# Other opening and drain of attention, gates in every second couple, and where the 64-bit conversions stand: a change to a fused attention and two-stage feed-forward kernel

## The chip, the cores and the metric

The kernel runs on one core of one Trainium2 chip. A core has a matrix engine (TensorE, PE in the profile, its weight loads apart as PEld), a vector engine (VectorE, DVE), a scalar engine (ScalarE, ACT), GpSimd (POOL) and a queue that mostly issues transfers (SyncE, SP). Each works through its own instructions in order and waits for the others through semaphores. SBUF is the working memory, PSUM takes TensorE's results. The metric is the device time of one execution, in microseconds (us).

## What is computed

Inputs are q, k, v (4 batches, 8 heads, 576 positions, head size 64), the weights of a mixture of 8 experts, and w_in and w_out, which arrive as 64-bit floating point numbers.

```python
scores = where((rel >= 0) & (rel < 128), scale * q @ k.T - slope[h] * abs(rel), -1e9)
attn   = exp(scores - max) / (sum + 1e-9);   x = attn @ v            # (2304, 512)
P      = exp(x @ w_gate - max);  8 times: P /= P.sum(1); P /= P.sum(0); P *= 2304 / 8
x      = sum over e of P[:, e] * (relu(x @ w1[e]) @ w2[e])           # 512 -> 1024 -> 512
h      = x @ w_in;   out = (h * cos(h)) @ w_out                      # 512 -> 2048 -> 512
```

## The kernel before

The program is one function, whose instructions are issued in an order written out by hand. Three stages follow each other.

**Attention** works on 16 pairs of heads. A pair has five groups of 128 queries (the last of 64), so there are 80 groups, and two groups that follow each other form a couple: 40 couples. In turn i of the loop (line 793) PE gets the scores of couple i (`emit_qk`, L537 and L535), then the products of couple i-4 (`emit_AV`, L639), transposes of q and k of the next pair (`emit_T`, L494) and the transposes of the probabilities of couple i-3 (`emit_PT`, L601 and L603). DVE takes the row maxima (`emit_max`, L547), ACT the exponentials (`emit_exp`, L562) and the copies of the transposed probabilities (L614), POOL normalizes (`emit_norm`, L586), and `emit_x` copies the finished x of a pair out of PSUM (L655 on DVE for odd pairs, L657 on ACT for even ones). PSUM has two score banks (`ps_s`), three banks for transposes (`ps_t`), one for gates and for the first halves of q and k (`ps_g`), and a double bank `xbank` for the products, whose second part the second halves of q and k use too. Couples 1 and 3 put half of their scores into `xbank`. Everything follows in program order on each engine; a buffer or a bank that is taken again makes the writer wait for its last reader.

Beside this, `side` spreads other work over the groups: `load_f64` and `convert_f64` (L260 to L279, five operations on DVE and one on ACT) turn a 128x512 piece of the 64-bit weights into fp32, one step a group; `prep_s`, `prep_a`, `prep_b` and `prep_sb` split expert weights into a high and a low part; `stages` and `combos` prepare the operands of the first expert block. `gates` puts the products x @ w_gate of 384 tokens (`gate_block`, L371) and, a turn later, their transposition by a matmul and the copy into `logits` (`gate_block2`, L380 and L381) into the loop. `load_heads` issues the loads of q, k and v on SP's queue.

**Three expert blocks** of 768 tokens follow, with 32 units each (8 experts times 4 slices). The products are a seven-product scheme: a unit computes its seven in the order 5, 1, 4, 2, 3, 6, 7 (`product`, L966); in the first block, the products with w2 of the unit before stand ahead of 7 (`batch`, L1194 to L1196, into the banks gT0 to gT2, evacuated by DVE). After each product and each tile, `slot` takes one step of every list of waiting work: `sbq` (here `prep_sb`, with POOL sums L181, an ACT copy L184, a DVE split L186), `bg` (late gates, then the normalization of P, `sinkhorn`, L389 to L423) and others. The first block starts with the late gates and `sinkhorn`, whose small matmuls (L393, L399, L417) stand among PE's products. **Three blocks of the last layer** end the program.

The conversions that attention doesn't take stand in `bg` of the second and third expert block.

## Time and profile before

| | us |
|---|---|
| median of 3 runs (lowest, highest) | 1987.18 (1985.54, 1992.14) |
| the profiled execution | 1983.78 |
| its span, first to last instruction | 1982.0 |

| engine | busy us | share of the span |
|---|---|---|
| PE | 1958.4 | 99% |
| PEld | 1823.2 | 92% |
| DVE | 1559.7 | 79% |
| ACT | 862.2 | 44% |
| POOL | 967.0 | 49% |

The profile is one execution. A row of the timeline gives the start, the duration, engine, line, operation, what is written and read by the program's names, and in brackets how long the engine was idle ahead of it and what released it. A matmul's end is modelled, so a busy PE isn't PE at its peak. A wait for several things is put down to the one that came last. Attention runs from 6.0 to 156.1 us.

### The profile page before, as it was taken

The numbers are of one execution on the slowest core, as the hardware profiler recorded it, in microseconds if no ns is written. First come the engines' busy times: TensorE is split into PE (matmuls) and PEld (weight loads), VectorE is DVE, ScalarE is ACT, GpSimd is POOL, SyncE is SP. The second block draws the span as 40 slices with busy tenths as digits, with TensorE's granted clock in tenths as the row PEclk, the third lists the DMA queues.
The fourth block names the chain that finished last, engine by engine and source line by source line (L and its number), as shares of the span: only waits on it lengthen the run. The fifth ranks groups of instructions, "written<-read, shape, count | busy, mean of one in ns | idle before, by whom it ended". The sixth has DMA issues, their size and how long they took to land.

```text
span 1982.0 us, 31160 instructions
## 1 busy us (share of the span) xinstructions
PE 1958.4 (99%) x10977; PEld 1823.2 (92%) x10977; DVE 1559.7 (79%) x2669; ACT 862.2 (44%) x1617; POOL 967.0 (49%) x939
## 2 busy tenths in 40 slices
PE   8999999999999999999999999999999999999999
PEld 6667899999999999999999999999999999998898
DVE  7885877777777788988988877888877776757766
ACT  6885444444444433333333433333233354554543
POOL 5673566666667545454536622545454523333221
PEclk9999999999999999999999999999999999999999
DMA  7854788888888999999999888999898765565552
GB/s 195 220 141 159 263 311 292 309 303 313 310 289 310 319 340 316 343 338 317 340 327 328 274 281 284 330 341 335 324 308 296 242 222 196 197 218 176 207 192 96
DMA packets 293755, 540.05 MB, mean 272 GB/s; under 512 B 80256, under 2 KB 141792, under 8 KB 286432
## 3 DMA queue, kind: packets, MB, share of 16 engines
q1 hardware_dynamic: 292240, 537.74, 78.6%
q8 instruction: 87, 1.43, 0.3%
q14 instruction: 68, 0.56, 0.1%
q10 hardware_dynamic: 1360, 0.33, 0.1%
HBM read 384.32 MB, written 153.67 MB: 271 GB/s over the span
## 4 chain that ended last, share of the span: by engine, by line
PE 88%; DVE 2%; DMA 1%; issue 0%; SPq 0%; POOL 0%; ACT 0%; ACTq 0%; DVEq 0%; POOLq 0%
PE gT L1105 23%; PE y_moe L966 19%; PE z_moe L966 10%; PE gT L1195 7%; PE gT L1196 7%; PE gT L1194 7%; PE y_ffn L966 5%; PE x_moe L966 5%; PE z_ffn L966 2%; PE x_ffn L966 1%; DMA wbX<-wdp 1%; SPq L96 0%; DVE waX L145 0%; DVE acc_ffn L1175 0%; DVE ta L939 0%
## 5 line engine op out<-in xcount | busy, mean ns | idle before, releaser
L1105 PE MATMUL gT<-hX,wbX 128*128 128x384 f32 x2688 | 538.3, 334 | 0.9 <-DMA wbX<-wdp 0.5
L1105 PEld LDWEIGHTS gT<-hX,wbX 128*128 128x128 f32 x2688 | 471.7, 188 | 3.5 <-DMA wbX<-wdp 1.5
L966 PE MATMUL y_moe<-xtT_moe,waX 128*128 128x384 f32 x1728 | 347.1, 335 | 0.6 <-ACT s_moe L995 0.6
L966 PEld LDWEIGHTS y_moe<-xtT_moe,waX 128*128 128x128 f32 x1728 | 304.3, 188 | 3.7 <-ACT s_moe L995 0.9
L1117 DVE TENSOR_TENSOR acc_moe<-gT,acc_moe 128x384 f32<-128x384 f32 x432 | 237.7, 550 | 77.7 <-PE gT L1105 76.0
L1196 PE MATMUL gT<-wbX,hX 128*128 128x512 f32 x660 | 258.0, 391 | 0.0
L1195 PE MATMUL gT<-wbX,hX 128*128 128x512 f32 x660 | 257.8, 391 | 0.0
L1194 PE MATMUL gT<-wbX,hX 128*128 128x512 f32 x660 | 257.7, 390 | 0.0
L995 ACT ACTIVATE s_moe<-y_moe 128x384 f32<-128x384 f32 x192 | 93.3, 486 | 345.6 <-PE y_moe L966 345.5
L1139 POOL TENSOR_TENSOR hodd<-hodd 128x384 f32<-128x384 f32 x128 | 155.4, 1233 | 139.4 <-DVE hX L1125 70.4
L1139 POOL TENSOR_TENSOR cX<-cX 128x384 f32<-128x384 f32 x128 | 146.6, 1165 | 153.6 <-DVE hX L1125 93.8
L955 POOL TENSOR_TENSOR hX<-cX,hX 128x768 fp32r<-128x768 f32 x44 | 83.5, 1914 | 249.3 <-ACT hX L952 208.6
L132 POOL TENSOR_TENSOR s<-ra 128x256 f32<-128x256 f32 x80 | 62.4, 780 | 251.3 <-DVE waX L145 178.9
L1185 DVE SCALAR_TENSOR_TENSOR acc_moe<-gT,prob,acc_moe 128x512 f32<-128x512 f32 x174 | 129.6, 747 | 37.6 <-PE gT L1196 35.8
L1196 PEld LDWEIGHTS gT<-wbX,hX 128*128 128x128 f32 x660 | 123.8, 188 | 26.0
L1194 PEld LDWEIGHTS gT<-wbX,hX 128*128 128x128 f32 x660 | 123.9, 188 | 25.4 <-DVE acc_ffn L1175 0.6
L1195 PEld LDWEIGHTS gT<-wbX,hX 128*128 128x128 f32 x660 | 123.9, 188 | 24.5
L911 ACT ACTIVATE hX<-cX 128x768 fp32r<-128x768 f32 x64 | 44.0, 687 | 218.7 <-DVE cX L998 218.7
L1125 DVE TENSOR_TENSOR hX<-cX,hX 128x768 fp32r<-128x768 f32 x112 | 132.4, 1182 | 1.1 <-ACT hX L1129 1.1
L1125 DVE TENSOR_TENSOR hX<-hodd,hX 128x768 fp32r<-128x768 f32 x112 | 127.5, 1138 | 0.9 <-ACT hX L1129 0.9
L966 PE MATMUL z_moe<-xtT_moe,waX 128*128 128x384 f32 x576 | 116.4, 335 | 0.4 <-DVE waX L145 0.2
L966 PE MATMUL z_moe<-xtB_moe,waX 128*128 128x384 f32 x576 | 115.9, 335 | 0.0
(210 smaller groups left out, 3771.9 us busy)
## 6 DMA issues: line engine op xcount, KB each, us to landing
waX<-wd SPq DMA_DIRECT2D x264, 512.0 KB, 5.5
wbX<-wdp SPq DMA_DIRECT2D x224, 512.0 KB, 6.5
wd<-waX SPq DMA_DIRECT2D x32, 1792.0 KB, 6.8
wdp<-sb SPq DMA_DIRECT2D x32, 1024.0 KB, 5.8
wdp<-wbX SPq DMA_DIRECT2D x96, 256.0 KB, 4.4
wbX<-wd SPq DMA_DIRECT2D x24, 1024.0 KB, 4.8
waX<-wd SPq DMA_DIRECT2D x88, 256.0 KB, 5.2
ra<-in_moe_w_dram SPq DMA_DIRECT2D x64, 256.0 KB, 7.4
```

What stands on the lines that cost most here:

```text
L132: nc.gpsimd.tensor_tensor(out=s4[:, o], in0=x, in1=y, op=op)
L955: eng.tensor_tensor(out=h[:, 1], in0=c, in1=h[:, 0].bitcast(F32), op=ALU.subtract)
L966: nc.tensor.matmul(ps[:, :HB], wa[:, WI[m], wl, kc, :], x[:, xl, kc, :], start=start and kc == 0 and n_ == 0, stop=stop and kc == 1 and n_ ...
L995: nc.scalar.activation(out=t["s", i], in_=ps[:, :HB], func=AF.Copy)
L1105: nc.tensor.matmul(ps[:, :HB], w[:, u, wl, d * P:(d + 1) * P], x[:, xl, u, :], start=m in (1, 5, 2) and n_ == 0, stop=m in (4, 3, 2) and n ...
L1117: nc.vector.tensor_tensor(out=a, in0=ps[:, :HB], in1=a, op=ALU.add)
L1125: nc.vector.tensor_tensor(out=x[:, 1], in0=H[:, q], in1=x[:, 0].bitcast(F32), op=ALU.subtract)
L1139: nc.gpsimd.tensor_tensor(out=H[:, t[0], c], in0=H[:, t[1], c], in1=H[:, t[2], c], op=ALU.subtract)
L1185: nc.vector.scalar_tensor_tensor(out=a, in0=ps, scalar=pe, in1=a, op0=ALU.mult, op1=ALU.add)
L1194: nc.tensor.matmul(ps, hf[f][:, 0, ts], wb[:, f, 0, :], start=f == 0, stop=False)
L1195: nc.tensor.matmul(ps, hf[f][:, 0, ts], wb[:, f, 1, :], start=False, stop=False)
L1196: nc.tensor.matmul(ps, hf[f][:, 1, ts], wb[:, f, 0, :], start=False, stop=f == 1)
```

## The change

- **Opening.** Couple 1's scores take two banks of `ps_t`, couple 3's the ordinary score banks; neither uses `xbank`. In turn 0 the loads of q and k of pair 2 are issued, and the v loads of pairs 0 and 1 move behind them; afterwards q and k are loaded for pair + 3 instead of pair + 2. In turn 3 `emit_PT` stands right behind the gates, ahead of `emit_AV` and the transposes of q and k.
- **Drain.** In turns 41 to 43 `emit_PT` stands ahead of `emit_AV` too. In the last four groups the second head and the last, short group are normalized by DVE. The copies behind the transposes of groups 77 and 79 go to DVE. The last pair's x is copied half by ACT, half by DVE.
- **Gates.** A turn does either `gate_block2` or the next `gate_block`, not both.
- **Conversions.** None in attention (four before). Six stand in units 4 to 23 of the first expert block, one step behind each of the products 5, 1 and 7. 26 instead of 28 are left for the next two blocks.
- **`prep_sb(0)`** moves from the last turns of attention to the head of `sbq` in the first expert block.

```diff
@@ -522,10 +522,8 @@
         def emit_qk(n, pi, u):
             a = n % 2
             if n // 2 not in sbank:
-                if n // 2 in (1, 3):
-                    sbank[n // 2] = [xbank[:, :512], ps_t.tile([P, 512], F32, tag="t", name=f"s{n}_1")]
-                else:
-                    sbank[n // 2] = [ps_s.tile([P, 512], F32, tag="s", name=f"s{n}_{j}") for j in range(2)]
+                pool, tag = (ps_t, "t") if n // 2 == 1 else (ps_s, "s")
+                sbank[n // 2] = [pool.tile([P, 512], F32, tag=tag, name=f"s{n}_{j}") for j in range(2)]
             grp[n] = sbank[n // 2] if a == 0 else sbank.pop(n // 2)
             c0, c1 = span(u)
             k0 = (u - 1) * P + c0
@@ -583,7 +581,8 @@
                 c0, c1 = span(u)
                 for j in parts(u):
                     pt = grp[n][j]
-                    nc.gpsimd.tensor_scalar(
+                    eng = nc.vector if n >= NGR - 4 and (j or u == NG - 1) else nc.gpsimd
+                    eng.tensor_scalar(
                         out=pt[:, c0:c1], in0=pt[:, c0:c1], scalar1=rr[:, i:i + 1],
                         scalar2=1.0, op0=ALU.mult, op1=ALU.mult,
                     )
@@ -608,7 +607,7 @@
                 kk = min(P, S - t * P)
                 o = sb[:kk, :m].rearrange("p a q -> p (a q)")
                 i_ = bank.pop((pi, t))[:kk, :m, :].rearrange("p a q -> p (a q)")
-                if t == NG - 1:
+                if t == NG - 1 or n in (NGR - 3, NGR - 1):
                     nc.vector.tensor_copy(o, i_)
                 else:
                     nc.scalar.activation(out=o, in_=i_, func=AF.Copy)
@@ -651,7 +650,10 @@
                 t = b * S + c
                 m = min(S - c, TB - t % TB)
                 o = xr[t // TB][:, hp, t % TB:t % TB + m]
-                if pi % 2:
+                if pi + 1 == NP_ALL:
+                    nc.scalar.activation(out=o[:, :m // 2], in_=xp[:, c:c + m // 2], func=AF.Copy)
+                    nc.vector.tensor_copy(o[:, m // 2:], xp[:, c + m // 2:c + m])
+                elif pi % 2:
                     nc.vector.tensor_copy(o, xp[:, c:c + m])
                 else:
                     nc.scalar.activation(out=o, in_=xp[:, c:c + m], func=AF.Copy)
@@ -664,7 +666,6 @@
         load_heads(0, k, kraw, "kr", nc.scalar, part=1)
         load_heads(1, q, qraw, "qr")
         load_heads(1, k, kraw, "kr")
-        load_heads(0, v, vt, "v")
         make_identity(nc, ident)
         warm = ps_s.tile([P, 512], F32, tag="s", name="warm")
 
@@ -722,7 +723,6 @@
         distance(rel_li, rel_l, LW, hr)
         for t in qL:
             nc.gpsimd.memset(t, 0.0)
-        load_heads(1, v, vt, "v")
 
         groups = [(pi, u) for pi in range(NP_ALL) for u in range(NG)]
         done_tok = 0
@@ -730,8 +730,6 @@
         gate2 = []
         conv = []
         early = []
-        chunk = []
-        n_f64 = [0]
         wg_raw = ap_.tile([P, KC, E], F32, name="wg_raw")
         NGR = len(groups)
 
@@ -742,9 +740,9 @@
             if u < 4 and pi + 1 < NP_ALL:
                 emit_T(pi + 1, u, pool)
                 if u == 1:
-                    load_heads(pi + 2, q, qraw, "qr")
+                    load_heads(pi + 3, q, qraw, "qr")
                 if u == 3:
-                    load_heads(pi + 2, k, kraw, "kr")
+                    load_heads(pi + 3, k, kraw, "kr")
 
         def side(n):
             nonlocal conv
@@ -753,7 +751,7 @@
             if n == 2:
                 nc.sync.dma_start(out=wg_raw, in_=w_gate.rearrange("(k p) e -> p k e", p=P))
                 nc.gpsimd.memset(wg, 0.0)
-            if n == 3:
+            if n == 60:
                 load_f64(0)
             if 4 <= n < 8:
                 load_raw((n - 4) // 2, "ab"[n % 2])
@@ -763,28 +761,21 @@
                 conv += [prep_s(0), prep_a(0), prep_b(0), prep_s(1), prep_a(1), prep_b(1), prep_s(2)]
             if n == 48:
                 early.append(stages(("moe", 0), xr[0]))
-            if n == NGR:
-                conv.append(prep_sb(0))
             if n == 56:
                 early.append(combos(("moe", 0), xr[0]))
             if early and next(early[0], StopIteration) is StopIteration:
                 early.pop(0)
-            if 8 <= n < 50 and (chunk or n < 40):
-                if not chunk:
-                    chunk.append(convert_f64(n_f64[0]))
-                    n_f64[0] += 1
-                if next(chunk[0], StopIteration) is StopIteration:
-                    chunk.pop(0)
             if n % 2 == 0 or 44 <= n < 56 or n >= 72:
                 while conv and next(conv[0], StopIteration) is StopIteration:
                     conv.pop(0)
 
         def gates(n):
             nonlocal gate2, next_half
-            for j, lT in gate2:
-                gate_block2(j, lT, (ps_g, "g"))
-            gate2 = []
-            if n < NGR + 6 and next_half < 2 * NB and HB * (next_half + 1) <= done_tok:
+            if gate2:
+                for j, lT in gate2:
+                    gate_block2(j, lT, (ps_g, "g"))
+                gate2 = []
+            elif n < NGR + 6 and next_half < 2 * NB and HB * (next_half + 1) <= done_tok:
                 gate2.append((next_half, gate_block(next_half, (ps_g, "g"), ap_)))
                 next_half += 1
 
@@ -805,7 +796,14 @@
                 emit_exp(*pair(0)[0])
                 emit_T(0, 1, (ps_t, "t"))
                 emit_T(0, 3, (ps_g, "g"))
+                load_heads(2, q, qraw, "qr")
+                load_heads(0, v, vt, "v")
+                load_heads(2, k, kraw, "kr")
+                load_heads(1, v, vt, "v")
                 emit_max(*pair(0)[1])
+            if i == 3 or i > NGR // 2:
+                for g in pair(i - 3):
+                    emit_PT(*g)
             for g in pair(i - 4):
                 emit_AV(*g)
             if i == 1:
@@ -823,8 +821,9 @@
                     load_heads(pi + 2, v, vt, "v")
                     if pi % NPAIR == NPAIR - 1:
                         done_tok += S
-            for g in pair(i - 3):
-                emit_PT(*g)
+            if 3 < i <= NGR // 2:
+                for g in pair(i - 3):
+                    emit_PT(*g)
             if i < NGR // 2:
                 emit_norm(pair(i - 1))
             else:
@@ -1257,10 +1256,10 @@
         bg.append(late_gates())
         bg.append(sinkhorn((LastBank(), "m"), skp))
         bg.append(p_rows())
-        sbq.append(prep_sb(1))
+        sbq += [prep_sb(0), prep_sb(1)]
         fetch = []
         AHEAD = {1: (2, (5, 1)), 3: (2, (2, 3)), 7: (2, (6, 7)), 4: (1, (4,))}
-        chunk, ready = n_f64[0], 0
+        chunk, ready, spare = 0, 0, []
         queue = []
 
         def batch(ticks=1, tiles=range(TPB)):
@@ -1336,6 +1335,11 @@
                     slot()
                 elif (kind, b) == ("moe", 0) and u < UPE:
                     step_all(bg)
+                if (kind, b) == ("moe", 0) and m in (5, 1, 7):
+                    if not spare and UPE <= u < NU1 - 8:
+                        spare.append(convert_f64(chunk))
+                        chunk += 1
+                    step_all(spare)
                 for _ in range(pace.get(m, 0)):
                     next(nx, None)
             if pace is NEXT:
@@ -1353,6 +1357,7 @@
             while pre:
                 step_all(pre)
             assert (kind, b, u) != ("moe", 2, NU1 - 5) or ready == NU2 and not bg2
+            assert u != NU1 - 4 or not spare
         if queue[0] < len(steps) - 2:
             batch(tiles=range(GPB, TPB))
         product(steps[-1], 4)
```

PE's queue from the scores of group 4 on, before (`s6` are the scores of groups 6 and 7, `T2_0` and `T2_2` transposes of pair 2, `pt0` those of the probabilities of group 0):

```order
L494 MATMUL xbank_192<-ident_75,kr1_212 128x128 x3
L494 MATMUL T2_0_417<-ident_75,qr2_370 128x128 x2
L537 MATMUL xbank_192<-kT1_377,qT1_189 128x256
L537 MATMUL s6_1_435<-kT1_377,qT1_189 128x256
...
L494 MATMUL xbank_192<-ident_75,qr2_370 128x128 x3
L494 MATMUL T2_2_463<-ident_75,kr2_413 128x128 x2
L603 MATMUL pt0_468<-ident_75,sp_319 128x128
...
L537 MATMUL s8_0_491<-kT1_377,qT1_189 128x256
```

The same place of PE's queue after the change:

```order
L494 MATMUL xbank_192<-ident_75,kr1_212 128x128 x3
L494 MATMUL T2_0_423<-ident_75,qr2_329 128x128 x2
L535 MATMUL s6_0_441<-kT1_386,qT1_189 128x256
L535 MATMUL s6_1_442<-kT1_386,qT1_189 128x256
...
L602 MATMUL pt0_460<-ident_75,sp_311 128x128
...
L494 MATMUL xbank_192<-ident_75,qr2_329 128x128 x3
L494 MATMUL T2_2_480<-ident_75,kr2_337 128x128 x2
L535 MATMUL s8_0_498<-kT1_386,qT1_189 128x256
```

The six transposes `pt0` and `pt1` moved ahead of the transposes of q and k, and the scores `s6` left `xbank`.

The end of attention in PE's queue, before (`ptT72` are the copied probabilities of group 72, `v15` the values of the last pair):

```order
L639 MATMUL xbank_192<-ptT74_2622,v14_2457 64x128 x2
...
L601 MATMUL pt75_2626<-ident_75,sp_2534 128x128
L603 MATMUL pt76_2648<-ident_75,sp_2534 128x128
...
L639 MATMUL xbank_192<-ptT76_2653,v15_2552 64x256 x2
L639 MATMUL xbank_192<-ptT77_2660,v15_2552 64x256 x2
L601 MATMUL pt77_2655<-ident_75,sp_2582 128x128
...
L639 MATMUL xbank_192<-ptT78_2673,v15_2552 64x256 x2
```

And after the change:

```order
L600 MATMUL pt75_2578<-ident_75,sp_2486 128x128
L602 MATMUL pt76_2590<-ident_75,sp_2486 128x128
...
L638 MATMUL xbank_192<-ptT74_2574,v14_2409 64x128 x2
...
L600 MATMUL pt77_2597<-ident_75,sp_2534 128x128
...
L638 MATMUL xbank_192<-ptT76_2595,v15_2504 64x256 x2
L638 MATMUL xbank_192<-ptT77_2602,v15_2504 64x256 x2
L638 MATMUL xbank_192<-ptT78_2616,v15_2504 64x256 x2
```

The transposes of couples 38 (groups 76, 77) and 39 moved ahead of the products of the couple before, and the last two couples' products now follow each other.

DVE's queue at the start of the first expert block, before (`sb` is the w2 step's tile, `m1` and `m2` the maxima that `sinkhorn` starts with):

```order
L186 TENSOR_TENSOR sb_2638<-sb_2638 128x4x256
L381 COPY logits_82<-gT3_2732 128x24
L998 TENSOR_TENSOR cX_2728<-z_moe0_0_2733,s2_moe0_0_2795 128x384
L389 TENSOR_REDUCE m1_2799<-logits_82 128x1
...
L912 SCALAR_TENSOR_TENSOR hX_2727<-cX_2728,hX_2727 128x384
L395 TENSOR_REDUCE m2_2825<-gT3_2732 1x1
```

And after the change:

```order
L381 COPY logits_82<-gT3_2674 128x24
L997 TENSOR_TENSOR cX_2670<-z_moe0_0_2675,s2_moe0_0_2736 128x384
L389 TENSOR_REDUCE m1_2740<-logits_82 128x1
...
L911 SCALAR_TENSOR_TENSOR hX_2669<-cX_2670,hX_2669 128x384
L186 TENSOR_TENSOR sb_2684<-sb_2684 128x4x256
L395 TENSOR_REDUCE m2_2764<-gT3_2674 1x1
```

The split L186 moved from ahead of the last logits to the place right ahead of L395.

## Rows read from the trace of the kernel before

**Rows 1.** Busy by stage: length, then PE, PEld, DVE, ACT, POOL, clock, DMA share.

```profile
6.00:23.00 17.00, 12.70 (x79) 8.51 (x79) 11.57 (x59) 9.04 (x35) 6.38 (x18) 0.90 0.85 219
...
146.00:160.00 14.00, 11.82 (x96) 7.49 (x96) 4.31 (x16) 9.07 (x25) 9.43 (x18) 1.00 0.19 59
160.00:240.00 80.00, 75.82 (x395) 66.97 (x394) 60.08 (x132) 37.46 (x64) 30.64 (x34) 1.00 0.65 222
240.00:630.00 390.00, 389.98 (x1963) 353.54 (x1962) 300.83 (x401) 171.86 (x279) 254.74 (x232) 1.00 0.86 306
630.00:1590.00 960.00, 959.13 (x5495) 951.51 (x5494) 808.10 (x1206) 340.00 (x587) 461.69 (x409) 1.00 0.90 314
```

**Rows 2.** Waits of PE from 6 to 160 us: total us, times, longest.

```profile
PE xbank L639 <- ACT ptT L614: 3.4, 7, 0.9
PE xbank L494 <- DVE anb L547: 2.2, 2, 1.3
PE s L535 <- DVE anb L547: 1.2, 2, 0.7
PE T L494 <- DMA kr<-in_k_dram: 1.1, 2, 0.7
...
PE gT L371 <- DVE xr L655: 0.7, 1, 0.7
PE gate L371 <- DVE logits L381: 0.7, 1, 0.7
PE T L494 <- DVE logits L381: 0.6, 1, 0.6
```

**Rows 3.** Timeline of the opening on PE and PEld, couples 3 and 4.

```profile
15.19 0.28 PEld L537 LDWEIGHTS xbank<-kT,qT 64*128 64x128 f32 x1 [0.50 <-ACT kT L511]
...
18.43 0.55 PE L494 MATMUL xbank<-ident,qr 128*128 128x128 f32 x3 [1.33 <-DVE anb L547]
...
19.33 0.41 PE L494 MATMUL T<-ident,kr 128*128 128x128 f32 x2 [0.35 <-DMA kr<-in_k_dram]
...
20.33 0.70 PE L537 MATMUL s<-kT,qT 64*128 64x256 f32 x4
```

**Rows 4.** Busy and clock of a part of the opening, columns as in rows 1.

```profile
13.00:17.00 4.00, 3.71 (x17) 2.44 (x17) 2.22 (x14) 1.64 (x7) 2.70 (x8) 0.57 0.75 198
```

**Rows 5.** Groups by line, 6 to 160 us: longest and shortest operation of a conversion.

```profile
L267 DVE SCALAR_TENSOR_TENSOR fa<-f,fa 128x512 int32<-128x512 int32 x4 | 3.4, 851 | 0.0
...
L271 DVE TENSOR_SCALAR fb<-f 128x512 int32<-128x512 int32 x4 | 1.6, 396 | 0.0
```

**Rows 6.** Timeline of PE at couple 17.

```profile
64.82 0.59 PE L535 MATMUL s<-kT,qL 128*128 128x192 f32 x2 [0.53 <-DVE anb L547]
```

**Rows 7.** Timeline of the drain, PE's products and ACT's copies.

```profile
150.59 0.81 PE L639 MATMUL xbank<-ptT,v 128*64 128x128 f32 x12 [0.55 <-ACT ptT L614]
...
152.00 1.08 ACT L614 ACTIVATE ptT<-pt 128x512 f32<-128x512 f32 x2
...
152.65 1.14 PE L639 MATMUL xbank<-ptT,v 128*64 128x256 f32 x8 [0.22 <-ACT ptT L614]
...
154.95 1.25 PE L639 MATMUL xbank<-ptT,v 128*64 128x256 f32 x16 [0.36 <-ACT ptT L614]
...
156.13 1.34 PE L966 MATMUL z_moe<-xtT_moe,waX 128*128 128x384 f32 x6
```

**Rows 8.** Timeline of the first expert block's start, DVE, PEld and PE.

```profile
156.25 1.23 DVE L186 TENSOR_TENSOR sb<-sb 128x1024 fp32r<-128x1024 f32 x1 [1.27 <-ACT sb L184]
...
171.23 0.29 PEld L399 LDWEIGHTS gT<-m,ones 1*128 1x128 f32 x2 [0.25 <-DVE m L395]
...
192.42 0.51 PE L417 MATMUL gT<-prob,ones 128*128 128x144 f32 x2 [1.21 <-DVE prob L410]
```

**Rows 9.** Groups by line, DVE, 240 to 630 us: busy us, mean ns, idle before.

```profile
L186 DVE TENSOR_TENSOR sb<-sb 128x1024 fp32r<-128x1024 f32 x26 | 43.3, 1665 | 18.5 <-ACT sb L184 18.5
```

**Rows 10.** Timeline of DVE in a unit of the first expert block.

```profile
306.25 0.56 DVE L998 TENSOR_TENSOR cX<-z_moe,s_moe 128x384 f32<-128x384 f32 x1 [0.97 <-ACT s_moe L995]
```

## The prediction

> **What bounds the kernel now.** I read the table of stages first [rows 1]. TensorE (PE) is busy 389.98 of 390 us in the bulk of the first expert block and 959.13 of 960 in the next two, so nothing that is taken off VectorE (DVE) or ScalarE (ACT) there can shorten them. PE has holes in three places only: the opening of attention (12.70 of 17 us), its drain (11.82 of 14 us) and the start of the first expert block (75.82 of 80 us). Second, the waits of PE inside attention and its handover [rows 2]: these seven rows add up to 9.9 us, and no releaser dominates. A change that is worth anything must remove waits out of this list, and 9.9 us plus a little is about all there is to win. Since PE is the bound afterwards, a microsecond won here stays won to the end of the span.
>
> **Opening.** Couple i (two groups of 128 queries) runs scores, row maxima, exponentials, transposes, products. In couple 3 PE finishes the scores at 17.10 (18.43 less its wait of 1.33), then stands until the maxima are taken, because the next transposes of q go into xbank, which holds half of these scores [rows 3]. After the change couple 3's scores lie in the ordinary score banks, xbank is free, and the six probability transposes of couple 0 stand ahead of the q transposes, so there is something to do as well. The next transpose waits another 0.35 for k; that load is now issued ahead of both v loads. From 17.10 to the scores of couple 4 at 20.33 is 3.23 us, of which 1.68 are these two waits; the work between is the same, so 1.55 remain. The other wait on maxima, 2.2 in total less 1.33, thus 0.9 at couple 1 [rows 2], goes for the same reason, but the work behind it waits on DVE, which does not become earlier by as much: I count half, 0.4. The first half of couple 3's scores no longer needs ScalarE's copy out of xbank, for which its weight load waits 0.50 at 15.19 [rows 3]: 0 to 1, I take 0.5. The price: couple 3 now waits for the maxima of couple 2, since there are two score banks; DVE takes these before, so I count nothing, and up to 0.5 if it is late. Opening: 1.7 + 0.4 + 0.5 = **2.6 us**, bounds 1.0 and 4.3.
>
> The clock is the reason for the upper bound. Between 13 and 17 us the granted clock is 0.57 on the mean [rows 4], that is 1.2 GHz for most of it, behind a stretch of short work and waits. PE is busy 3.71 us there, so at 2.4 GHz some 1.7 us of it would be saved, if the path is PE's own. The Trainium skill (TensorE: Matmul & The Clock Gate, Part 1) says that the throttled clock is the default and activity releases it. By that a fuller opening could keep the clock up and the opening would be worth about 4; what is filled here stands mostly behind the slow stretch, so I keep 2.6.
>
> **Loads of q and k.** They are now fetched three head pairs ahead, into the buffer that the pair just transposed leaves. PE waits on k twice, 1.1 in total, 0.35 of it counted above [rows 2, 3]: **0.7 us** (0.5 to 0.8). The loads now wait for PE's transposes at the head of SP's queue, and v loads, expert weights and the stores stand behind them; PE reaches the transposes soon after the issue, and all of those are needed couples later. If that cover were gone, one load would be late by about what k was, 0.7.
>
> **Conversions out of attention.** Four conversions, of five DVE operations of 396 to 851 ns [rows 5], are 8 to 17 us of DVE time. But DVE isn't what PE waits for in most couples: in the stretch with conversions one wait on maxima stands out, 0.53 at 64.82 [rows 6], and of the 3.4 us on ScalarE's copies [rows 2] most lie outside. I take 0.8, bounds 0.3 and 2. In the first expert block the six conversions take 30 such operations, 12 to 26 us, against 89 us in which DVE is idle there [rows 1]; DVE waits 0.97 us for ScalarE in every unit just where they are put [rows 10]. Covered, so 0. The two conversions that the later blocks lose gain nothing, as PE does not wait there.
>
> **Gates.** A transposed gate and the next gate stood in one couple and shared one bank; PE waited 0.7 and 0.6 for the copy of the logits [rows 2]. Now they alternate: gate 2 comes a couple later. **1.2 us**, bounds 0.5 and 1.3, as ScalarE's copy of a gate still has to clear the bank.
>
> **Drain.** At the end each product waits for ScalarE's copy of the transposed probabilities, which waits for the transposes just ahead of it: 150.59, 152.65 and 154.95, with 0.55, 0.22 and 0.36 us of idle [rows 7]; two copies take 1.08. After the change the transposes of couples 38 and 39 stand ahead of the products of 37 and 38, so that a copy lies beside 0.81 to 1.14 us of products, half of the copies and half of the normalizing go to DVE, idle there. The three waits are 1.13: **1.2 us**, bounds 0.4 (normalizing bounds the chain) and 2.2 (PE's sequencer gaps go too). Then the last block of x is copied by two engines and no longer stands behind the 1.23 us split of w2 on DVE [rows 8]; the first late gate waited 0.7 for it [rows 2]: **0.7 us**, bounds 0.3 and 0.7.
>
> **What the moved w2 step costs.** prep_sb(0) leaves the drain and goes ahead of prep_sb(1) in the expert block's queue. Its DVE split (1.23 us) and the ScalarE copy that feeds it now stand directly ahead of L395, the maximum for which PE already waits 0.25 at L399 [rows 8]. Nothing covers it: 1.5 us lost (1.0 to 1.8). Against it, the splits that follow slide too, and the one that stood ahead of the column sums at 192.42, where PE waits 1.21, moves behind them: I count 0.9 of that back, bounds 0 and 1.2. Net **0.6 us lost**, bounds 1.8 lost and 0.2 won.
>
> **Sum.** 2.6 + 0.7 + 0.8 + 1.2 + 1.2 + 0.7 - 0.6 = 6.6 us. Against the profiled execution, 1983.78 us (span 1982.0): 1977.2. The median of the three runs shown is 1987.18, 3.4 above the profiled one; against it 1980.6, which is my figure.
>
> **Rivals.**
> *Chains that stay* (0.26). In the opening and drain every wait has a second one behind it: DVE's order in the opening is unchanged, and the normalizing sets the drain. Then of 2.6 and 1.2 only 1.0 and 0.4 are left, conversions give 0.3, and the moved split costs 1.8 in full: 1.0 + 0.7 + 0.3 + 1.2 + 0.4 + 0.7 - 1.8 = 2.5, so 1984.7. For it speaks that the waits on DVE and ScalarE lie within one couple; against it that DVE is busy 4.31 of 14 us in the drain.
> *All waits go* (0.10). The clock stays up as well, and DVE's slack takes the rest of the ScalarE waits: 4.3 + 0.7 + 2 + 1.3 + 2.2 + 0.7 - 0.2 = 11, so 1976.2.
> *Conversions starve the first expert block* (0.08). DVE evacuates the three product banks there; a conversion step ahead of an evacuation holds PE. The same split takes 1.23 us at 156 us and 1665 ns on the mean in the block [rows 8, 9], where GpSimd (POOL) works, so an operation of a conversion may take about a third more there: 30 of 0.53 to 1.15 us. It decides once the step is longer than DVE's idle time before it, 0.97 [rows 10]; if two thirds of 30 steps of 0.9 reach PE, 18 us are lost: 1987.2 - 6.6 + 18 = 1998.6. Against it: the steps stand behind products 5, 1 and 7, not within the tiles. The Trainium skill (SBUF — State Buffer, "SBUF: two separate sides") says that a DVE operation with two SBUF inputs and a GpSimd operation lock each other out for a whole instruction. The longer split agrees, 1.67 against 1.23. By that rule a step would wait up to a whole GpSimd instruction, and this rival is where that would end.
> That the order isn't changed as described is excluded by the order itself; it shows each of the moves.
>
> **How the numbers follow.** Forecast 0.56, with a range of its own from 5 to 9 us won (1978 to 1982). The range leaves out the starved block and the outer half of the two other rivals: 1976.5 to 1986.0. About 0.3%, here 6 us, is what a measurement of this kernel can tell from no change, and the forecast is only just beyond it. Faster by more: 0.48 out of the forecast and 0.10 from the case in which all waits go, 0.58. Within: 0.08 of the forecast, 0.26 and 0.02 of the starved block, 0.36. Slower: 0.06.
>
> **What would show it.** In the profile of the changed kernel: the scores of couple 4 start near 17.7 instead of 20.33; the waits of transposes on k, on maxima for xbank and of gates on logits are gone from PE's list; the first expert product starts 5 to 7 us before 156.13 [rows 7]; the wait at L399 grows to about 1.7; DVE's share in 240 to 630 rises by 3 to 7 points with PE still full. It is wrong if PE shows waits on DVE between 240 and 560, if xbank is still waited for in couple 3, or if the waits removed come back one step later under another name.

## The result, and the profile after

The changed kernel takes 1998.55 us (median of 6 runs, 1995.81 to 2001.2) against 1986.36 us for the kernel before in the same runs: 1.006 times as long, 95% interval 1.0042 to 1.0077. It is slower by 0.6%, and lies outside the range. Its profiled execution has a span of 1995.4 us, 13.4 more than before.

Lines of the changed file stand one lower than before from L911 on (L912 is now L911, L995 is L994, L998 is L997, L1196 is L1195). Busy time by stage of the changed kernel, columns as in [rows 1]:

```profile
6.00:23.00 17.00, 14.58 (x111) 10.10 (x107) 14.32 (x74) 12.89 (x48) 8.19 (x23) 1.00 0.79 192
146.00:160.00 14.00, 13.07 (x104) 9.92 (x101) 4.00 (x10) 4.08 (x9) 2.59 (x4) 1.00 0.00 1
160.00:240.00 80.00, 73.97 (x369) 65.64 (x368) 63.30 (x133) 39.34 (x66) 36.81 (x39) 0.98 0.70 241
240.00:630.00 390.00, 381.68 (x1896) 343.54 (x1895) 328.34 (x418) 169.04 (x274) 254.69 (x224) 0.99 0.87 308
630.00:1590.00 960.00, 955.74 (x5468) 947.44 (x5468) 799.40 (x1189) 335.40 (x580) 453.27 (x407) 1.00 0.90 313
```

The opening is fuller than in [rows 1], as meant; the second row is no measure of the drain, since the first expert product now starts at 149.64 and most of the row is expert block. But PE now has holes where it had next to none (0.0 and 0.9 us before): 8.3 us in the first expert block's bulk, 4.3 in the next two blocks. Its waits from 160 to 690 us in the changed kernel (total us, times, longest) say what it stands for:

```profile
PE gT L1195 <- DVE hX L911: 8.3, 4, 2.1
PE gT L1193 <- DVE acc_moe L1174: 2.0, 1, 2.0
PE gT L417 <- DVE prob L410: 1.7, 1, 1.7
PE gT L399 <- DVE m L395: 1.3, 1, 1.3
PE z_moe L965 <- DVE waX L145: 0.9, 1, 0.9
```

PE does the same products in the same order in both kernels from the first expert product on, so one can subtract the starts of one and the same product. That gives the ledger of the change, in us later (+) or earlier (-) than in the first profile of before; all kernels of this study are in it, by the names that the experiments below have (e1 and so on). The columns are places, by their time in the kernel before: the first expert product, the end of the handover from attention, the end of the stretch with the stalls, and the last unit.

| Kernel | 156.13 us | 236.14 us | 530.76 us | 1960.77 us |
|---|---|---|---|---|
| the changed kernel | -6.5 | -2.9 | +9.8 | +13.5 |
| the same, second profile | -4.4 | -1.2 | +13.1 | +15.3 |
| before, second profile | -1.0 | -1.0 | -1.0 | -0.1 |
| e1 conversions only | -3.0 | -2.6 | +10.0 | +15.5 |
| e14 load alone | -0.7 | -0.4 | +12.3 | +15.1 |
| e2 no conversions in block | +1.0 | +4.6 | +4.6 | +3.8 |
| e17 the same, GpSimd in quarters | -1.3 | +2.1 | +2.1 | +3.1 |
| e3 first split back | -6.1 | -5.9 | +6.8 | +14.9 |
| e4 GpSimd in quarters | -5.9 | -2.5 | +0.4 | +2.9 |
| e5 step behind product 6 | -5.5 | -1.6 | -1.5 | +2.0 |
| e9 four conversions | -5.3 | -2.1 | +5.9 | +10.0 |
| e10 combined | -5.6 | -4.9 | -4.9 | -1.8 |
| e12 combined and quarters | -5.5 | -5.0 | -4.8 | -0.3 |

So in the first profile of the changed kernel attention won 6.5 us, the handover lost 3.6 of it, the bulk of the first expert block lost 12.7, and the rest 3.7; in the second it is 4.4, 3.2, 14.3 and 2.3.

**One of the four stalls.** Timeline of the changed kernel's VectorE (DVE), GpSimd (POOL) and PE; start, duration, line, and the wait before it:

```profile
298.06 0.90 DVE L911 SCALAR_TENSOR_TENSOR hX<-cX,hX 128x384 fp32r<-128x384 f32 x1 [0.59 <-ACT hX L910]
298.89 0.96 DVE L271 TENSOR_SCALAR fb<-f 128x512 int32<-128x512 int32 x1
299.88 1.11 DVE L275 SCALAR_TENSOR_TENSOR fb<-f,fb 128x512 f32<-128x512 uint32 x1
300.91 1.76 DVE L186 TENSOR_TENSOR sb<-sb 128x1024 fp32r<-128x1024 f32 x1
302.60 2.87 DVE L279 SCALAR_TENSOR_TENSOR fb<-fb,fa 128x512 f32<-128x512 f32 x1
305.38 0.54 DVE L911 SCALAR_TENSOR_TENSOR hX<-y_moe,hX 128x384 fp32r<-128x384 f32 x1
...
301.56 3.35 POOL L161 TENSOR_TENSOR wbX<-rb,wbX 128x1024 fp32r<-128x1024 f32 x1
...
319.77 2.40 POOL L161 TENSOR_TENSOR wbX<-rb,wbX 128x1024 fp32r<-128x1024 f32 x1
...
305.98 0.50 PE L1195 MATMUL gT<-wbX,hX 128*128 128x512 f32 x1 [2.07 <-DVE hX L911]
```

In attention, where the kernel before had them, the two operations of a conversion that matter below took 660 and 514 ns on the mean (groups of before, 6 to 160 us, busy us and mean ns):

```profile
L279 DVE SCALAR_TENSOR_TENSOR fb<-fb,fa 128x512 f32<-128x512 f32 x4 | 2.6, 660 | 0.0
L260 DVE TENSOR_SCALAR fa<-f 128x512 int32<-128x512 int32 x4 | 2.1, 514 | 0.1
```

Here L279 takes 2.87 us. It starts 1.0 us into POOL's subtraction L161, and ends 0.6 us, about its own length, behind L161's end at 304.91. The hX that PE needs for the next tile (L911) stands right behind it. L161 itself is long because L186 ran when it came: 2.40 us at 319.77, where nothing is in its way, 3.35 here. Three conversion steps in one unit bring the third of them to this place; that happens four times in the six conversions, and these are the four waits of 2.07 us. The mean of the groups from 240 to 630 us hides it (busy us, mean ns):

```profile
L275 DVE SCALAR_TENSOR_TENSOR fb<-f,fb 128x512 f32<-128x512 uint32 x6 | 10.4, 1734 | 0.1
L279 DVE SCALAR_TENSOR_TENSOR fb<-fb,fa 128x512 f32<-128x512 f32 x6 | 10.4, 1734 | 0.1
L267 DVE SCALAR_TENSOR_TENSOR fa<-f,fa 128x512 int32<-128x512 int32 x5 | 6.1, 1222 | 0.0
L260 DVE TENSOR_SCALAR fa<-f 128x512 int32<-128x512 int32 x5 | 4.8, 966 | 0.0
```

Of the 12.7 us only 8.3 are these waits. After two of the four PE went on at half clock (1.2 GHz) for a while; two stalls and the stretch behind each (columns as in [rows 1], the clock is the last figure but two):

```profile
303.00:306.00 3.00, 0.93 (x5) 0.40 (x4) 3.00 (x3) 0.34 (x1) 3.00 (x2) 1.00 1.05 394
306.00:310.00 4.00, 4.00 (x18) 3.30 (x19) 3.75 (x6) 2.62 (x4) 0.79 (x2) 1.00 1.01 307
352.00:355.00 3.00, 0.92 (x5) 0.44 (x4) 3.00 (x3) 0.22 (x1) 2.93 (x2) 1.00 1.05 392
355.00:359.00 4.00, 4.00 (x12) 3.15 (x13) 3.02 (x5) 2.62 (x4) 0.74 (x1) 0.62 0.99 313
```

By the starts of the products the four stalls cost 2.4, 4.0, 4.0 and 2.3 us: 4.0 where half clock followed. Which ones it follows is not the program's doing: in the second profile of the same kernel it is the first, third and fourth (granted clock 0.59, 0.66 and 0.63 over 4 us behind them), and the four cost 4.0, 2.4, 4.0 and 4.0.

### The profile page after: what moved, and what is told of

It reads as the page before. It is cut to its first block, busy times and chain, and to the rows that moved or that the text cites. A ratio compares the mean times of both kernels' runs of the same rounds, so it can differ in the third digit from the quotient of the medians.

```text
span 1995.4 us, 31149 instructions
## 1 busy us (share of the span) xinstructions
PE 1961.6 (98%) x10977; PEld 1825.3 (91%) x10977; DVE 1586.5 (80%) x2675; ACT 861.6 (43%) x1616; POOL 965.1 (48%) x935
## 4 chain that ended last, share of the span: by engine, by line
PE 87%; DVE 5%; DMA 3%; POOL 2%; issue 1%; ACT 1%; SPq 0%; POOLq 0%; DVEq 0%; ACTq 0%
PE gT L1104 23%; PE y_moe L965 17%; PE z_moe L965 9%; PE gT L1195 7%; PE gT L1194 6%; PE gT L1193 6%; PE y_ffn L965 5%; PE x_moe L965 4%; PE z_ffn L965 2%; PE xbank L638 2%; DMA wbX<-wdp 1%; PE x_ffn L965 1%; PE s L535 1%; DVE waX L145 1%; DMA wdp<-wbX 1%
## 5 line engine op out<-in xcount | busy, mean ns | idle before, releaser
L1195 PE MATMUL gT<-wbX,hX 128*128 128x512 f32 x660 | 260.3, 394 | 8.3 <-DVE hX L911 8.3
L1193 PE MATMUL gT<-wbX,hX 128*128 128x512 f32 x660 | 259.8, 394 | 2.0 <-DVE acc_moe L1174 2.0
L994 ACT ACTIVATE s_moe<-y_moe 128x384 f32<-128x384 f32 x192 | 93.3, 486 | 350.7 <-PE y_moe L965 350.6
L1195 PEld LDWEIGHTS gT<-wbX,hX 128*128 128x128 f32 x660 | 125.0, 189 | 36.4 <-DVE hX L911 10.0
L1193 PEld LDWEIGHTS gT<-wbX,hX 128*128 128x128 f32 x660 | 125.1, 190 | 28.1 <-DVE acc_moe L1174 2.4
```

What stands on the lines that cost most here:

```text
L994: nc.scalar.activation(out=t["s", i], in_=ps[:, :HB], func=AF.Copy)
L1193: nc.tensor.matmul(ps, hf[f][:, 0, ts], wb[:, f, 0, :], start=f == 0, stop=False)
L1195: nc.tensor.matmul(ps, hf[f][:, 1, ts], wb[:, f, 0, :], start=False, stop=f == 1)
```

## The experiments

**Conversions only (e1).** The kernel before, with the conversions moved as in the change:

```diff
-            if n == 3:
+            if n == 60:
                 load_f64(0)
-            if 8 <= n < 50 and (chunk or n < 40):
...
+                if (kind, b) == ("moe", 0) and m in (5, 1, 7):
...
+                    step_all(spare)
```

> The kernel before, with one part of the change alone: no conversion in attention, six in the first expert block at the places of the changed kernel; attention's opening, drain, gates and loads stay as they were. Theory A (a conversion operation that meets GpSimd's 128x1024 subtraction stands until that ends and holds PE): four operations of about 2.86 us, four waits of PE of 2 us at the unit products in 240 to 630 us, two of them followed by a stretch at half clock; 11 to 14 us lost in that stretch, some 1 us won in attention, so about 1997. Rival B (the loss belongs to the new attention order, which starts the expert block 6.5 us earlier with its weights not yet there): the first expert block stays without waits, within 2 us of before, about 1986.

Measured 1999.19 us, ratio 1.0068 (1.0056 to 1.008). PE waits four times for hX, 8.3 us in total, and the bulk loses 12.7. The conversions alone cost all that the change costs. Attention won 3.0, not 1, and the later blocks lost another 5.5, which I had not expected.

**The change without the conversions in the block (e2).** The conversion code as before, the rest as changed.

> The changed kernel with the conversions as they were before: four in attention, none in the first expert block. Theory A: PE is full again from 240 to 630 us, attention ends some 1 us later than in the changed kernel (149.6 us becomes about 150.5); what is left is the new attention (5 to 6 won) and the start of the expert block (3.6 lost): 2 to 3 us below before, about 1984. Rival B: the loss stays where it is, about 1998.

Measured 1988.77 us, ratio 1.0017 (1.0006 to 1.0028). PE is busy 390.00 of 390 us again, so rival B is out. But attention ended 1.0 us *later* than before, and the time is 5 above what A expected. At one operation 3.1 us of lead at couple 16 turn into 2.8 of lag at couple 19. Timeline of this kernel's DVE, POOL and PE:

```profile
74.58 2.50 DVE L260 TENSOR_SCALAR fa<-f 128x512 int32<-128x512 int32 x1 [2.13 <-DMA f<-in_moe_w_out_dram]
...
74.46 2.35 POOL L161 TENSOR_TENSOR wbX<-rb,wbX 128x1024 fp32r<-128x1024 f32 x1
...
77.91 1.26 PE L535 MATMUL s<-kT,qT 64*128 64x256 f32 x7 [2.73 <-DVE anb L545]
```

The same POOL operation, met in attention: 2.50 us in place of 0.51 on the mean, the row maxima wait behind it, PE waits 2.73, and the granted clock from 80 to 86 us is 0.50.

**GpSimd in quarters (e4).** The direct test of the mechanism: no DVE operation moves.

```diff
-            nc.gpsimd.tensor_tensor(out=wb[:, :, 1], in0=rb, in1=wb[:, :, 0].bitcast(F32), op=ALU.subtract)
+            for f in range(2):
+                for o in (0, FU):
+                    x = wb[:, f, 1, o:o + FU]
+                    nc.gpsimd.tensor_tensor(out=x, in0=rb[:, f, o:o + FU], in1=wb[:, f, 0, o:o + FU].bitcast(F32), op=ALU.subtract)
```

> The changed kernel, where GpSimd's subtraction of a w2 block (128x1024, 2.4 us alone) is made in four operations of 128x256; every operation of VectorE stands where it did. Theory A (an operation of VectorE stands for the rest of the GpSimd operation that it meets, whole): no conversion operation is longer than about 1.5 us, PE's four waits of 2.07 us shrink to 0.5 or vanish, and 8 to 12 us come back, about 1988. Rival E (VectorE simply has too much ahead of the copy that PE needs, whatever GpSimd does): the waits stay within 0.3 of 2.07 and the time within 2 us of the changed kernel, about 1998.

Measured 1987.27 us, ratio 1.0013 (1.0004 to 1.0021). The same place in this kernel (its lines stand three higher), timeline of DVE, POOL and PE:

```profile
302.97 1.23 DVE L282 SCALAR_TENSOR_TENSOR fb<-fb,fa 128x512 f32<-128x512 f32 x1
304.12 0.54 DVE L914 SCALAR_TENSOR_TENSOR hX<-y_moe,hX 128x384 fp32r<-128x384 f32 x1
...
301.92 4.25 POOL L164 TENSOR_TENSOR wbX<-rb,wbX 128x256 fp32r<-128x256 f32 x4
...
304.71 0.50 PE L1198 MATMUL gT<-wbX,hX 128*128 128x512 f32 x1 [0.44 <-DVE hX L914]
```

The step is 1.64 us shorter and the wait is 1.63 shorter, 0.44 in place of 2.07, four times. The half clock is gone too. The bulk loses 2.9 instead of 12.7. Rival E is out.

**The step behind product 6 (e5).** `m in (5, 1, 7)` becomes `m in (5, 6, 7)`; POOL as in the change.

> The changed kernel, where the conversion step behind product 1 stands behind product 6 instead; as many steps and operations as before, only this third step of a unit goes behind the sums that PE waits for, and GpSimd stays as it was. Theory A (what costs is the one step that meets GpSimd's 128x1024 subtraction ahead of the sum that PE needs): no operation of 2.86 us and no wait of 2.07 us from 240 to 630 us, 10 to 13 us back there, time about 1987. Rival E (VectorE has too much to do in a unit, wherever it stands): the waits of PE move to another line and stay above 5 us in total, time above 1993.

Measured 1984.69 us, ratio 0.9993 (0.9984 to 1.0001): as long as before. There is no wait of PE from 240 to 630 us. The third step still meets POOL (1.51 us at 305.34), but behind the sums. The sums themselves run inside the same POOL operation and are as short as ever; timeline of DVE and POOL:

```profile
303.95 0.54 DVE L911 SCALAR_TENSOR_TENSOR hX<-y_moe,hX 128x384 fp32r<-128x384 f32 x1
304.41 0.54 DVE L997 TENSOR_TENSOR cX<-x_moe,s_moe 128x384 f32<-128x384 f32 x1
...
305.34 1.51 DVE L279 SCALAR_TENSOR_TENSOR fb<-fb,fa 128x512 f32<-128x512 f32 x1
...
302.90 3.40 POOL L161 TENSOR_TENSOR wbX<-rb,wbX 128x1024 fp32r<-128x1024 f32 x1
```

The sums read one input from PSUM (y_moe, x_moe); L279 reads both from SBUF, and ends 0.55 us behind L161's end at 306.30. DVE has 329.61 us of work there, as in the changed kernel, and PE is full:

```profile
240.00:630.00 390.00, 390.00 (x1963) 353.56 (x1963) 329.61 (x431) 173.73 (x282) 266.12 (x232) 1.00 0.90 317
```

So it was never the amount of work on DVE.

**The quarters in attention (e17).** The kernel of the second experiment with the quarters.

> The changed kernel with the conversions in attention, as in the earlier run of that name (where attention ended 1.0 us later than before the change, with one wait of 2.7 us at couple 17 behind a conversion operation of 2.50 us, and half clock after it), but GpSimd's 128x1024 subtraction made in quarters. Theory A (that operation stood for GpSimd's): no conversion operation of attention is longer than 1.5 us, the wait at couple 17 is below 1.2 us, and attention ends 3 to 6 us earlier than in that run, at 151 to 154 us; the whole time about 1984. Rival K (the late load of the 64-bit weights, for which that operation had waited, is what cost there): attention ends within 1 us of that run's 157.1.

Measured 1987.0 us, ratio 1.0005 (0.9996 to 1.0014). No conversion operation is longer than 0.93 us, and the wait at couple 17 is 1.10. From couple 16 to 19 this kernel loses 1.5 us where the other lost 5.9, which is theory A. But attention ended only 2.3 us earlier, not 3 to 6, and the whole time is 3 us above the 1984 expected, because attention is 2.1 us slower by couple 12; the second profile of the changed kernel, below, shows such a difference between two executions of one program, and whether that is the reason here was not tried.

**The first split back in the drain (e3).**

```diff
+            if n == NGR:
+                conv.append(prep_sb(0))
-        sbq += [prep_sb(0), prep_sb(1)]
+        sbq.append(prep_sb(1))
```

> The changed kernel with the first w2 split back in attention's drain, where it was before. Theory C (the moved split costs the expert block's start 3.6 us: 1.3 at the maximum of L399, the rest because its store to DRAM is queued among the loads and ScalarE, which waits for it before the next split, holds the evacuations behind it): waits of PE from 150 to 240 us fall back to those of before, and the time is 2.5 to 3.5 below the changed kernel, about 1995.5. Rival D (the block's start loses because it starts earlier, ahead of its weights): no gain, or a loss of up to 1, as the split then stands in the drain again.

Measured 1996.69 us, ratio 1.0057 (1.0045 to 1.0069). The handover now loses 0.2 us, not 3.6, so theory C holds there. What the moved split costs besides L399 stands in the waits of ScalarE (ACT) from 160 to 240 us, first of the changed kernel, then of before, and in the landing time of the store of unit 1's split (issued at 177.92 and at 165.12; KB each, us to landing), in the same order:

```profile
ACT sb L184 <- DMA wdp<-sb: 4.6, 1, 4.6
...
ACT sb L184 <- DMA wdp<-sb: 1.8, 1, 1.8
...
wdp<-sb SPq DMA_DIRECT2D x1, 1024.0 KB, 9.8
...
wdp<-sb SPq DMA_DIRECT2D x1, 1024.0 KB, 5.0
```

There is one buffer sb. In the changed kernel unit 0's own store, issued at 165.02, lands after 5.3 us and holds nothing up. But unit 1's split has slid back with it, to 175.20. Its store is on the way together with the store of w1 (issued at 175.20) and the next loads, and lands after 9.8 us; ACT stands 4.6 us for it in front of unit 2's split, and the evacuations behind it come late: PE waits 1.97 at 191.58 (L1193), and the granted clock from 190 to 200 us is 0.83. In this experiment ACT has no such wait. But the whole time is not 2.5 to 3.5 below the changed kernel (ratio 1.0057 against 1.006): by the ledger the later blocks lost 8.1. PE waited longer for weights in the second block, 5.7 us, and went on at half clock behind two of the three waits.

**Four conversions in place of six (e9)** (`and chunk < 4` added to the condition).

> The changed kernel with four conversions in the first expert block in place of six, so that 28 are left for the later blocks as before the change. Theory F (the waits of PE on the weights' way back from DRAM in the second block, 2 to 5 us in the kernels with six and none with four done early, come because the feed-forward weights are prepared some 40 us earlier and their transfers fall on that block): no such wait above 0.5 us from 640 to 1600 us, which gives back 2 to 3 us there, beside the 6 us of the two conversions that go; time about 1990. Rival G (those waits come from the shift in time alone): they stay at 2 us or more, and the time is about 1993.

Measured 1993.76 us, ratio 1.0041 (1.0029 to 1.0053): two stalls left, each costing 4.0, with half clock behind both. The waits for weights from 640 to 1600 us did not go, so theory F falls in that form. These rows are from this kernel, from the first and second profiles of before, and from the second of the changed kernel (whose first has 4.1 us there):

```profile
PE gT L1104 <- DMA wbX<-wdp: 4.2, 3, 1.8
...
PE gT L1105 <- DMA wbX<-wdp: 0.5, 1, 0.5
...
PE gT L1105 <- DMA wbX<-wdp: 1.7, 2, 1.0
...
PE gT L1104 <- DMA wbX<-wdp: 2.9, 2, 2.2
```

Rival G, the shift in time alone, fits this run (some 1993 was said for it), but the shift alone does not order the ledger: e10, 4.9 us early, waits 3.2 us there, and e2, 4.6 us late, does not wait.

So both kernels were profiled a second time (e15, e16), unchanged:

> The kernel before, unchanged, for a second profile. Theory J (the waits of PE on weights from DRAM in the second block, 0.5 us in the first profile of before and 2 to 6 us in most of the later kernels, change from one execution to the next of the same program): here too they may be anything from 0 to 5 us, and the time is within 3 us of 1986. Theory F or G (they belong to early conversions, or to the shift in time): they are 0.5 us again.

> The changed kernel, unchanged, for a second profile. What belongs to the program repeats: four waits of 2.07 us and 1.3 us at the maximum of L399, 6 us won in attention within 1. Theory J: the waits on weights from DRAM in the second block, 4.0 us in the first profile (one of them at the end of the first block), differ by 1 us or more. Theories F and G: they repeat within 0.5.

Measured 1983.67 and 1999.13 us. The four waits (8.3 us) and the 1.3 at L399 repeat. The waits for weights differ by 1.2 us between two executions of one program, as J said. Attention won 4.4, not 6.5: 2.0 went in the opening, at couples 5 and 6, behind a wait of 1.6 us and at a granted clock of 0.73 from 34 to 38 us. So a figure of 2 us or less that rests on one profile of each of two kernels may be such a difference; where one stands below, it is a reading and not shown.

**The load alone (e14).** In the kernel of the first experiment `n == 60` goes back to `n == 3`.

> The kernel of the run with the conversions alone (conversions in the first expert block, attention otherwise as before the change), with one thing put back: the load of the first 512 KB of 64-bit weights is issued in couple 1 again, though nothing in attention uses it. Theory H (the 2.0 us that the opening won without conversions are this load's, which shares the DMA engines with k and v and so makes the slow stretch of 13 to 17 us): the first products of probabilities start at 21.5 us again, not at 19.24, and the granted clock of 13 to 17 us is 0.57 again. Rival I (the conversion's own operations on VectorE and ScalarE cost them): 19.2 us stays, and the clock stays at 1.0. The whole time differs by 2 us at most from 1999.

Measured 2000.85 us, ratio 1.0077 (1.0063 to 1.0091). The first products of probabilities start at 21.22 us, not at 19.24; 13 to 17 us without the load and with it (columns as in [rows 4]):

```profile
13.00:17.00 4.00, 2.33 (x17) 1.47 (x16) 3.17 (x18) 1.64 (x7) 3.40 (x9) 1.00 0.83 197
...
13.00:17.00 4.00, 3.28 (x17) 2.29 (x17) 2.62 (x15) 1.86 (x9) 2.59 (x7) 0.66 0.81 207
```

As many products (x17), at full clock without the load, and with it at half for much of the time (0.66 on the mean; 0.57 in [rows 4]). The other profiles with attention's old order and the load are the two of before: first products at 21.48 and 21.19, clock 0.57 and 0.61. So theory H holds for the old order: 2.0 us of the opening belong to the load, though nothing there uses it. Not all of that is the clock: 1.0 is there already at the scores in front of the slow stretch, at 13.62 against 12.62. How the load reaches PE was not tried. In the new order the price isn't there at that place: e2 and e17 have the load early too, with the first products at 16.98 and 16.94, against 17.07 in the changed kernel, and a granted clock of 1.00 from 13 to 17 us.

**Combined**, first without (e10) and then with the quarters (e12):

> The changed kernel with three edits together: the first w2 split back in attention's drain, four conversions in place of six, the conversion step behind product 6 instead of 1. If the three prices are what the runs so far say (3.1 at the start of the expert block, 12.5 in its bulk, 2 to 3 in the second block), the new attention's 6 us are left: about 1980, faster than before by 0.3%. If the losses only change place, it stays at 1986 or above.

> The combined kernel (first w2 split in the drain, four conversions, step behind product 6), with GpSimd's 128x1024 subtraction in quarters as well. If that operation costs only where VectorE meets it ahead of a needed sum, nothing is left for the quarters to win in the first block, and four starts in place of one cost nothing that PE sees: within 2 us of the combined kernel's 1981.5. If it also slows the second block's or the start's splits, up to 3 us less, about 1979.

Measured 1981.45 us, ratio 0.9982 (0.9974 to 0.9991), and 1982.08 us, ratio 0.998 (0.9971 to 0.9989). The prices are the right ones: with the split in the drain, four conversions and the step behind product 6, the bulk is without a wait (lag -4.9 throughout), and this kernel is faster than the kernel before by 0.2%, and than the changed one, by the two ratios, by 0.8%. The later blocks still lose 3.0 us. The quarters add nothing once nothing needed stands behind the long operation.

## Why the prediction was wrong

**Where it was right.** Attention: I summed 2.6 + 0.7 + 0.8 + 1.2 + 1.2 + 0.7 = 7.2 us; the two profiles show 6.5 and 4.4. The waits I named are gone from PE's list (no transpose waits for k, for maxima at xbank, or for logits; one late gate still waits 0.3 for logits), and the scores of couple 4 start at 15.86, earlier than the 17.7 that I gave. Some came back under other names, which I had given as a sign of being wrong (changed kernel, 6 to 160 us):

```profile
PE xbank L638 <- ACT ptT L613: 2.2, 4, 0.9
PE s L535 <- ACT sp L560: 1.6, 1, 1.6
PE xbank L638 <- DVE anb L545: 1.3, 1, 1.3
```

**The step that failed** is "Covered, so 0" under the conversions. I compared sums: 12 to 26 us of operations against 89 us of idle DVE time. But DVE works in order, and the price is set by what stands behind one operation and how long that one can get. In the rival I took the length from the mean of L186 [rows 9], a third more than alone [rows 8], and stretched all 30 operations by it. The stretch is no factor: it is the rest of the POOL operation that is met. Beside POOL's 128x256 operations that made 0.66 into 1.22 us, beside L161 2.86. I had not looked for the longest POOL operation in the unit, 2.4 us. The trace of before shows one such meeting, hidden in a mean: the 851 ns of L267 [rows 5] are three operations of about 0.67 us and one of 1.40, which ends 0.55 us behind POOL's L161 (timeline of before, DVE and POOL):

```profile
79.26 1.40 DVE L267 SCALAR_TENSOR_TENSOR fa<-f,fa 128x512 int32<-128x512 int32 x1
...
77.76 2.35 POOL L161 TENSOR_TENSOR wbX<-rb,wbX 128x1024 fp32r<-128x1024 f32 x1
```

The Trainium skill (SBUF — State Buffer, "SBUF: two separate sides") states a lock for the whole instruction between a GpSimd operation and a VectorE operation with two SBUF inputs or in a mode that uses two ports, and I had weighed it, as the rival's mechanism, at 0.08. The trace agrees with it for the two-input L279, 2.87 us, which ends 0.6 behind POOL's operation; the one-input L260, 2.50 us and 0.3 behind, falls under it only if it is in such a mode, which no run here shows.

**The starved block** was that rival, at 1998.6; 1998.55 was measured, which is partly chance. It counted 20 steps of 0.9 us, 18 in all. It was four operations of 2.86 us, 8.3 us of waits, and 4.4 behind them, most of it at half clock behind two, plus 3 us more at the handover than I had summed and 3.7 later. What I held against it, "the steps stand behind products 5, 1 and 7, not within the tiles", is wrong in DVE's order: the step behind product 1 stands ahead of an hX (L911) that the next tiles need.

**The moved split** was 0.6 us in my sum and is 3.4 at the handover (3.6 less the 0.2 that stay when it is put back). The term at L399 was right in kind (1.31 us of wait against 0.25 [rows 8], where I added 1.5). The 0.9 that I counted back at the column sums came too: the wait of 1.21 at L417 is gone in the first profile, and down to 0.58 in the second. What I left out is that unit 1's split slides as well: its store, 1 MB from the only buffer, lands after 9.8 us, and the next split needs the buffer. That is the wait of 1.97 at L1193 with the lower clock behind it.

**Conversions out of attention** were 0.8 and are 3.0 by the first experiment: 2.0 for the load of the first 512 KB in the opening, for which I had no term, and 1.0 at couples 13 and 18. In the new order they would cost more, 7.5 between one profile of e2 and one of the changed kernel, mostly by the long operation at couple 17.

**The others**, from the starts of the couples' products in the changed kernel less those of the first experiment: opening with the loads of q and k 1.6 (3.3 summed), on top of the 2.0 of the load; gates 0.8 (1.2 summed); drain and last copy 1.1 (1.9 summed). Load and order don't add up, as each takes away the slow stretch from 13 to 17 us: with the load still early, e2's opening is 3.1 us ahead of before by couple 12 (1.0 in e17). All these come from one profile each. In the sum of the case in which all waits go I took 0.2 off for the moved split, where my bound was 0.2 won: it should be 11.4 us and 1975.8. **Of the later blocks** I said that nothing changes; PE lost 3.7 there, mostly waiting for weights.

**What stays open** is that last item. Kernels with early conversions in the first expert block waited 2.9 to 5.7 us for those weights, before and the two with conversions in attention 0 to 2.4; one program varies by 1.2. That early conversions cause some of it is possible and not shown; with four in place of six the waits stayed.

## What to carry to other kernels

An idle share does not cover a step on an engine that works in order: look at the one thing behind each new operation, and at the longest operation of the engine it can collide with, here GpSimd's for a VectorE step that reads SBUF alone; read maxima, not means. Best here was to put the step behind what the bound engine needs (the bulk lost 0.0 us in e5); cutting GpSimd's operation in pieces came next (2.9 in e4). And a moved step takes its loads and stores along, and pushes back those of its neighbours: here the load was worth 2.0 us in the old order of the opening, and the late store a wait of 1.97 us (1.57 in the second profile).

## What the runs showed of the hardware

VectorE operations whose inputs lie in SBUF alone (L279, L275, L267) and that met GpSimd's L161 stood until it ended, and it did not need two tensor inputs: the one-input L260 took 2.50 us in place of 0.51. Operations with an input from PSUM were not held: in the changed kernel 48 of the sums L911 and L997 started inside an L161 with at least 0.6 us of it to go, and took 0.54 to 0.56 us, as elsewhere. It goes both ways, L161 took 3.35 us in place of 2.40 behind L186. A wait of PE of 2.07 us was followed by half clock in two of four cases in one profile of the changed kernel, and in three of four in the other (the third alone in both); a wait of 2.73 by about 6 us of it.
